# Another order of the first two head pairs: score banks for the second pair's transposes, VectorE for the first pair's low parts, k on ScalarE's queue

## The chip, the cores and the metric

The kernel runs on one core of a Trainium2 chip. The metric is the device time of one execution in microseconds (us). TensorE (PE) multiplies matrices, VectorE (DVE), ScalarE (ACT) and GpSimd (POOL) work on elements, SyncE (SP) issues transfers. Each engine works through its own list of instructions in order and waits on semaphores of the others.

## The reference

```python
# attention in clusters: q, k, v of 2 batches x 8 heads x 768 rows x 64
q_assign = argmax(einsum('bhsd,hcd->bhsc', q_n, c_n))      # 16 clusters; rows are normalised
k_assign = argmax(einsum('bhsd,hcd->bhsc', k_n, c_n))
mask = q_assign[:, :, :, None] == k_assign[:, :, None, :]
scores = where(mask, scale * q @ k.T, -1e9)
attn = exp(scores - max) / sum ; attn_out = attn @ v
x = attn_out as 1536 x 512
h = x @ w_in ; x = (h - tanh(h)) @ w_out                   # d_ff 2048
out = (sigmoid(x @ w_gate) * (x @ w_val)) @ w_out          # d_ff 1536
```

## The kernel before, in words

Sixteen heads are worked on as eight pairs; after them come the two feed-forward blocks. Every factor is split into a high part (rounded to the format that TensorE reads at full rate) and a low part (the rest), and a product is the sum of high x high, high x low and low x high.

`pair_prep` (a pair's preparation) loads q and k of two heads (L717), transposes them on TensorE (L728), copies the transposed halves to SBUF on ScalarE (`evac`, L732), and multiplies them by the normalised centroids on TensorE (`score`, L782). VectorE turns these cluster scores into one-hot rows (`assign`, L791 to L802), and TensorE transposes the one-hot rows (L873 in the first pair, L833 later). For the first pair ScalarE writes the high parts (`cast`, L746) straight into the operand tile of each head, `stk`, and POOL subtracts them for the low parts (L751); ScalarE adds the one-hot rows (L877). For later pairs high and low parts go to `hlq` and `hlk` (L758, L768) and SP copies them into `stk` (L466). v is scaled by a power of two (`v_scale`, L681 to L689, L923, L926).

A head's scores stand in a bank of PSUM ("big": `ba`, `bb`, later `bc`), one bank for each 128 rows, six in a head. A head is treated in one of two ways by the digit in `TURN`. Head 0 has digit 1: scores (L1013), maximum on VectorE (L1021), two exponentials on ScalarE (L1016, to float32 and to float16), the low part on POOL or VectorE (L1032), a transposing transfer (L1035), and the product with v (L1044 to L1046). All other heads first get their maxima from a product of high parts alone (`head_max`: L946 on TensorE, L950 on VectorE), which are turned into a row (L959, L965), and then scores with the maximum subtracted (L1066), exponentials (L1069), the low part (L1080) and the product with v (L1092 to L1094).

Small results use four other banks of PSUM: `smr` (three slots, in use at the start, the first NR pairs) and `sm`. When the last user of `smr` is done (`ramp`, `first_over`), its banks become the third big bank `bc` and one more `sm`. `keep_busy` (L659) puts matmuls on a tile of zeros into TensorE's list; they compute nothing that is used.

The order of all this is made when the program is built: a planner gives every task a place by a table of due times (`ORDER`, some 3,500 numbers), the look-ahead of each engine (`AH_...`) and the free tiles. A task takes its tile from the slot whose name is in its `take`. So a changed table moves every instruction, while what is computed stays.

The feed-forward blocks take their results from halved banks (`over_left`, `over_right`, `sm`); their products are L1379 and L1742, and with EU=1 the first ones are recorded one by one (L1446). `pair_of` splits results into high and low parts, a share GV or GW of the low parts on VectorE; W1L, D1L, W2L and D2L say how early weights are loaded.

```python
    for i in range(N_BUSY):
        fill.append(add(PE, 0.111, 1e6, keep_busy, fill[-1:], tail=0.055))
...
        smk = "smr" if s < NR else "sm"
...
            both = Slot("big") if s < PRM["TB"] else None
...
                on_v = x < PRM["NDV"]
```

Of the kernel before, what the change touches and what calls it, by code (L numbers as in the profile page):

```python
# [26 lines left out]
PRM = dict(  # L27
    QUEUE=2.4, AH_PE=0.1219, AH_ACT=0.29, AH_DVE=0.0344, AH_POOL=5.5247, AH_SP=2.0746, N_BUSY=110, NR=2, NRH=1,
    HX=['hx', 'hhxx'], WAR=0.8, LM=9, LV=9, ZP1=-12.307, ZP=1.419, FD=0.1631, FO=0.8005, LOQ=0, VHI=0,
    ZV0=-23.288, VR=40.471, ZSV=-53.844, ZRAW=10.895, ZT=1.445, ZH=70.02, ZHL=13.774, ZS=6.68, ZC=-1.658,  # L30
    ZOT=-19.503, ZD=22.333, ZDH=1.004, ZDM=4.532, ZVL=13.784, ZVS=23.559, ZX=-17.9, ZE=25.348, ZLOW=35.365,
    ZLOWP=0.736, SEMS=1.0, TC=0.58, TW=0.9, M2=1, ZQK=0.347, ZMS=-68.272, Z0=47.754, HB=93.143, NB4=5,
    ROWS=0.0155, NHA=8, RAWL=1.6, NMID=2, NPL=2, XB=0, XT=1, GV=0.1258, GW=0, NPL2=1, W1L=0.556, D1L=0.31,
    W2L=1.628, D2L=-0.119, ZI=18.277, ZJ=-10.865, PORT=0.12, PVG=1, NSPL=1, NRE=1.056, TURN='1000000000000000',
    ZMX=20.689, ZTR=9.194, TRL=2.05, TRC=1.4, ZPT=0.419, PVT=2, HD=0, HDO=0.0751, HC=0, HCO=0, ZHC=-56.991,
    NAT=2, TB=1, ZN=2.791, ZNL=-12.734, NDV=0, EU=1, ZUD=-29.266, ZU=-22.481, ZUS=-19.807, NEW=0, ZEW=-3.275)
# [1909 lines left out]
```

## Time and profile before

| | |
|---|---|
| time, median of 3 runs | 777.66 us (776.62 to 778.03) |
| profiled execution | 776.54 us, span 774.8 us |
| TensorE busy | 767.1 us (99%), 5905 matmuls |
| VectorE, ScalarE, GpSimd busy | 568.4, 457.6, 569.9 us |
| matmuls on zeros (L659) | 220, 16.6 us busy |

A matmul's end is modelled, and the next one starts before it, so a group's busy time and the distance of its starts are two things: six score products of 128 rows by 384 columns last 1.3 us in the timeline, and the next instruction starts about 1.1 us after the first. Times in the views count from the start of the span. The profiled execution is longer than its span by 1.8 us, and 1.1 us below the median of the runs.

### The profile page before, as it was taken

The page shows a single profiled execution, that of the slowest core. Times are in us where ns is not written, and L with a number is a line of the kernel's source. Part 1 is how long each engine was busy: PE and PEld are TensorE (multiplying, and loading weights), DVE is VectorE, ACT ScalarE, POOL GpSimd, SP SyncE. Part 2 cuts the span into 40 slices and gives each one's busy share as a digit, 9 for nine tenths or more (in the row PEclk, how much of TensorE's full clock was granted, in tenths as well). Part 3 has the DMA queues.
Part 4 walks back from the last instruction along what each step waited for, and adds up shares of the span by engine and source line. Part 5 has one row for each costly group of instructions (what it writes and reads, how often), then busy time and mean ns, then how long its engine had stood idle before and what let it go on. Part 6 is the DMA issues. An engine that isn't in the chain of part 4 may idle for free.

```text
span 774.8 us, 15780 instructions
## 1 busy us (share of the span) xinstructions
PE 767.1 (99%) x5905; PEld 725.4 (94%) x5905; DVE 568.4 (73%) x1111; ACT 457.6 (59%) x881; POOL 569.9 (74%) x604
## 2 busy tenths in 40 slices
PE   8999999999999999999999999999999999999998
PEld 7888999898899999999999999999998989899996
DVE  6797888788987977868577787795475796756324
ACT  6689997889996644644445455665552636254240
POOL 7368977878889874978778799698693888668231
PEclk9999999999999999999999999999999999999999
DMA  4797666575632100312122232012230242211004
GB/s 104 183 195 156 138 154 141 125 153 136 162 115 66 46 1 28 123 55 86 40 94 69 96 106 72 0 49 91 67 96 19 78 130 89 82 41 41 1 1 163
DMA packets 75572, 69.58 MB, mean 90 GB/s; under 512 B 39252, under 2 KB 60072, under 8 KB 75496
## 3 DMA queue, kind: packets, MB, share of 16 engines
q1 hardware_dynamic: 75352, 68.55, 33.0%
q8 instruction: 46, 0.75, 0.4%
q14 instruction: 30, 0.25, 0.1%
q10 hardware_dynamic: 144, 0.03, 0.0%
HBM read 45.12 MB, written 3.15 MB: 62 GB/s over the span
## 4 chain that ended last, share of the span: by engine, by line
PE 93%; DVE 3%; ACT 1%; issue 1%; DMA 1%; SPq 0%; DVEq 0%; ACTq 0%
PE over_left L1379 23%; PE over_left L1742 21%; PE over_right L1379 7%; PE over_right L1742 6%; PE sm L1379 6%; PE sm L1742 4%; PE bc L1066 3%; PE sm L782 2%; PE ba L1066 2%; PE bb L1066 2%; PE sm L1092 2%; PE sm L1093 2%; PE sm L1094 2%; PE ba L946 2%; PE bb L946 1%; PE sm L659 1%
## 5 line engine op out<-in xcount | busy, mean ns | idle before, releaser
L1080 POOL TENSOR_TENSOR pt<-pf,pt 128x768 f16<-128x768 f32 x46 | 77.5, 1695 | 17.7 <-ACT pf L1069 6.6
L1742 PE MATMUL over_left<-xh,stk 128*128 128x384 f32 x228 | 70.8, 336 | 0.0
L1762 DVE TENSOR_TENSOR pf<-over_left,pf 128x384 f32<-128x384 f32 x62 | 34.3, 554 | 40.2 <-ACT pf L1758 24.5
L1080 POOL TENSOR_TENSOR ptt<-pf,ptt 128x768 f16<-128x768 f32 x29 | 49.5, 1713 | 13.2 <-ACT pf L1069 10.8
L1410 ACT ACTIVATE hlk<-pf 128x384 fp32r<-128x384 f32 x44 | 22.9, 523 | 35.7 <-POOL pf L1772 13.7
L1379 PE MATMUL over_left<-hlk,w 128*128 128x384 f32 x154 | 43.4, 336 | 0.0
L1379 PE MATMUL over_left<-stk,w 128*128 128x384 f32 x138 | 43.2, 337 | 0.0
L1092 PE MATMUL sm<-vs,pt 128*128 128x65 f16 x318 | 42.9, 194 | 0.0
L1742 PEld LDWEIGHTS over_left<-xh,stk 128*128 128x128 f32 x228 | 42.3, 188 | 0.5
L1093 PE MATMUL sm<-vs,pt 128*128 128x64 f16 x318 | 42.8, 195 | 0.0
L1094 PE MATMUL sm<-vs,pt 128*128 128x65 f16 x318 | 42.4, 191 | 0.0
L1742 PE MATMUL over_left<-sum,stk 128*128 128x384 f32 x166 | 41.8, 336 | 0.2 <-ACT pf L1758 0.2
L1742 PE MATMUL over_left<-xh,ry 128*128 128x384 f32 x124 | 39.9, 336 | 0.0
L950 DVE TENSOR_REDUCE finr<-ba 128x1 fp32r<-128x768 f32 x35 | 33.2, 948 | 6.6 <-PE ba L946 3.9
L1412 POOL TENSOR_TENSOR hlq<-pf,hlk 128x384 fp32r<-128x384 f32 x25 | 25.8, 1032 | 16.1 <-ACT hlk L1410 16.1
L1758 ACT ACTIVATE pf<-over_left 128x384 f32<-128x384 f32 x44 | 21.4, 488 | 27.1 <-PE over_left L1742 27.1
L1379 PE MATMUL over_left<-w,stk 128*128 128x512 f32 (+1 forms) x108 | 37.0, 391 | 0.0
L1742 PE MATMUL over_left<-xl,stk 128*128 128x384 f32 x110 | 36.9, 336 | 0.0
L1497 DVE TENSOR_TENSOR ptt<-over_left,ptt 128x384 f32<-128x384 f32 x58 | 31.5, 550 | 6.8 <-PE over_left L1379 6.8
L1066 PE MATMUL bc<-stk 112*128 112x384 f32 (+2 forms) x150 | 34.7, 354 | 0.2 <-DVE finr L950 0.2
L1092 PEld LDWEIGHTS <-pt 128*128 128x128 f16 x318 | 29.7, 96 | 5.3 <-issue 4.9
L1353 POOL TENSOR_TENSOR w<-vs,w 128x256 fp32r<-128x256 f32 x25 | 19.8, 803 | 20.1 <-ACT w L1351 20.1
(600 smaller groups left out, 3056.8 us busy)
## 6 DMA issues: line engine op xcount, KB each, us to landing
vs<-in_moe_w_out_dram SPq DMA_DIRECT2D x48, 256.0 KB, 2.7
vs<-in_moe_w_in_dram SPq DMA_DIRECT2D x24, 256.0 KB, 2.6
vs<-in_moe_w_val_dram SPq DMA_DIRECT2D x24, 256.0 KB, 2.7
vs<-in_moe_w_gate_dram SPq DMA_DIRECT2D x24, 256.0 KB, 2.8
stk<-hlq SPq DMA_DIRECT2D x28, 192.0 KB, 2.6
stk<-hlk SPq DMA_DIRECT2D x14, 384.0 KB, 4.5
rawq<-in_q_dram SPq DMA_DIRECT2D x16, 192.0 KB, 3.5
rawk<-in_k_dram SPq DMA_DIRECT2D x16, 192.0 KB, 3.9
```

The costliest lines, as they stand in the source:

```text
L946: nc.tensor.matmul(at(mx)[:, j, 0:HALF], at(sk)[0:km, 0, t * P:(t + 1) * P], at(sk)[0:km, 1, j * HALF:(j + 1) * HALF], start=True, stop=True)
L950: rd.append(use(mx, add(DVE, c_dve(S), z + t, lambda t=t, mx=mx: nc.vector.tensor_reduce(at(mh)[:, t:t + 1], at(mx)[:, :, 0:HALF], axis=AX ...
L1066: nc.tensor.matmul(o, at(sk)[0:n, l_, ts], at(sk)[0:n, m_, c], start=i == 0, stop=i == len(terms) - 1)
L1080: lambda nce=nc.vector if on_v else nc.gpsimd, pf=pf, pt=pt: nce.tensor_tensor(at(pt)[:, 1], at(pf), at(pt)[:, 0], op=ALU.subtract), [e0, ...
L1092: nc.tensor.matmul(oview()[:, t], ph, vv[:, 0:D + 1], start=(kt == 0), stop=False)
L1093: nc.tensor.matmul(oview()[:, t, 0:D], ph, vv[:, D + 1:2 * D + 1], start=False, stop=False)
L1094: nc.tensor.matmul(oview()[:, t], plo, vv[:, 0:D + 1], start=False, stop=(kt == T - 1))
L1379: nc.tensor.matmul(ps, a, b, start=(i == 0), stop=(i == n - 1))
L1412: nc.vector if on_v else nc.gpsimd).tensor_tensor(lo(), src(), hi(), op=ALU.subtract), [a], port=True)
L1497: u = add(DVE, c_dve(CH), z, lambda a=a, src=src: nc.vector.tensor_tensor(a(), src(), a(), op=ALU.add), [t] + prev)
L1742: nc.tensor.matmul(at(bank[to])[:, 0:CH], lh, rh, start=start and i == 0, stop=stop and i == 3 * KH - 1, skip_group_check=True)
L1762: return use(x, use(bank[n], add(DVE, c_dve(CH), rank[0], lambda: nc.vector.tensor_tensor(at(x), ps(n), at(x), op=ALU.add), deps)))
```

## The change

Many constants of the planner and the whole table `ORDER` are other numbers, and three places of the code are different. N_BUSY goes from 110 to 5 (220 matmuls on zeros become 10). NR goes from 2 to 1 and TB from 1 to 2: the second pair's transposes of q and k go to the big banks, and its cluster scores and one-hot rows to `sm`. NDV goes from 0 to 2: the first pair's four low parts are made on VectorE. The first pair's k is loaded from ScalarE's queue. Z01 exchanges the operand tiles of heads 0 and 1. PVT goes from 2 to 1, EU from 1 to 0. The sizes and the number of all other matmuls stay.

```diff
-    QUEUE=2.4, AH_PE=0.1219, AH_ACT=0.29, AH_DVE=0.0344, AH_POOL=5.5247, AH_SP=2.0746, N_BUSY=110, NR=2, NRH=1,
+    QUEUE=2.4, AH_PE=0.1324, AH_ACT=0.2649, AH_DVE=0.025, AH_POOL=4.8207, AH_SP=1.1014, N_BUSY=5, NR=1, NRH=1,
...
-    ROWS=0.0155, NHA=8, RAWL=1.6, NMID=2, NPL=2, XB=0, XT=1, GV=0.1258, GW=0, NPL2=1, W1L=0.556, D1L=0.31,
-    W2L=1.628, D2L=-0.119, ZI=18.277, ZJ=-10.865, PORT=0.12, PVG=1, NSPL=1, NRE=1.056, TURN='1000000000000000',
-    ZMX=20.689, ZTR=9.194, TRL=2.05, TRC=1.4, ZPT=0.419, PVT=2, HD=0, HDO=0.0751, HC=0, HCO=0, ZHC=-56.991,
-    NAT=2, TB=1, ZN=2.791, ZNL=-12.734, NDV=0, EU=1, ZUD=-29.266, ZU=-22.481, ZUS=-19.807, NEW=0, ZEW=-3.275)
+    ROWS=0.0155, NHA=8, RAWL=1.6, NMID=2, NPL=2, XB=0, XT=1, GV=0.0854, GW=0.0192, NPL2=1, W1L=1.109,
+    D1L=-0.243, W2L=1.563, D2L=-0.377, ZI=-4.342, ZJ=-2.662, PORT=0.12, PVG=1, NSPL=1, NRE=1.056,
+    TURN='1000000000000000', ZMX=19.248, ZTR=4.682, TRL=2.05, TRC=1.4, ZPT=-0.489, PVT=1, HD=0, HDO=0, HC=0,
+    HCO=0.0306, ZHC=-58.936, NAT=2, TB=2, ZN=-8.697, ZNL=-81.82, NDV=2, Z01=1, EU=0, ZUD=-40.578, ZU=-8.093,
+    ZUS=-38.353, NEW=0, ZEW=-20.328)
...
     nc.scalar.dma_start(cn, centroids.rearrange("h c d -> (h c) d"))
+    for hh in range(2):
+        nc.scalar.dma_start(tiles["rawk", 0][:, :, hh], k[0, hh].rearrange("(p t) d -> p t d", t=T))
     nc.scalar.activation(warm, warm, AF.Sqrt)
...
-            ld = add(SP, 2 * DMA_C, z + PRM["ZRAW"] + x - (90 if s == 0 else 0), lambda load=load: (load(0), load(1)),
+            ld = add(SP, 2 * DMA_C, z + PRM["ZRAW"] + x - (90 if s == 0 else 0), (lambda: None) if s == 0 and x else lambda load=load: (load(0), load(1)),
                      take=[raw], lat=PRM["RAWL"])
```

What this makes of the order is shown at three places. In the changed kernel's file the same lines stand 6 to 8 numbers lower (L728 is L722, L782 is L776, L946 is L940, L1013 is L1007). The first is the start of TensorE's list, the matmuls on zeros and the weight loads left out. `ba` and `bb` are big banks, `rawq` and `rawk` the loaded q and k, `cn` the centroids, `vm` and `e` the scale of v. Before:

```order
L728 MATMUL ba_76<-ident,rawq_121 128x128 x3
L728 MATMUL bb_80<-ident,rawk_124 128x128 x3
L728 MATMUL ba_76<-ident,rawq_121 128x128 x3
L728 MATMUL bb_80<-ident,rawk_124 128x128 x3
L647 MATMUL smr_84<-ident,cn 64x128
L685 MATMUL smr_85<-ident,vm 1x128
L782 MATMUL sm_71<-cb,xtk_125 128x96 x3
L782 MATMUL smr_84<-cb,xtq_122 128x96 x6
L782 MATMUL sm_71<-cb,xtk_125 128x96 x3
L687 MATMUL smr_85<-e,ones_167 128x2
```

In the changed kernel:

```order
L722 MATMUL ba_76<-ident,rawq_121 128x128 x6
L722 MATMUL bb_80<-ident,rawk_124 128x128 x6
L641 MATMUL smr_84<-ident,cn 64x128
L679 MATMUL smr_85<-ident,vm 1x128
L776 MATMUL sm_71<-cb,xtq_122 128x96 x6
L722 MATMUL ba_76<-ident,rawq_121 128x128 x6
L681 MATMUL smr_85<-e,ones_167 128x2
L776 MATMUL smr_84<-cb,xtk_125 128x96 x6
L722 MATMUL bb_80<-ident,rawk_124 128x128 x6
L776 MATMUL sm_72<-cb,xtq_122 128x96 x6
L776 MATMUL sm_72<-cb,xtk_125 128x96 x6
```

The second pair's twelve transposes and its scores now stand between the first pair's scores and its one-hot rows; before, they stood behind the first pair's one-hot rows. (Each score matmul of this list is two in the trace.)

The second place is VectorE's list in the changed kernel, from the first scale of v to the first one-hot rows (`oh`). Before, it went from the copies of the centroids (`cb`) to the scale of v (`e`) and on to the maxima (`mm`) of the cluster scores.

```order
L675 TENSOR_REDUCE vm<-rawv_92 128x1
L646 COPY cb<-smr_84 64x4x16 x2
L745 TENSOR_TENSOR stk_86<-xtq_122,stk_86 64x768
L745 TENSOR_TENSOR stk_87<-xtq_122,stk_87 64x768
L670 TENSOR_REDUCE e<-smr_85 1x1
L671 TENSOR_SCALAR e<-e 1x1
L672 TENSOR_SCALAR e<-e 1x1
L673 RECIPROCAL e<-e 1x1
L745 TENSOR_TENSOR stk_87<-xtk_125,stk_87 64x768
L745 TENSOR_TENSOR stk_86<-xtk_125,stk_86 64x768
L683 TENSOR_SCALAR sv<-smr_85 128x1
L785 TENSOR_REDUCE mm_127<-sm_71 128x12
```

The four low parts (L745) now stand ahead of the first pair's assignment.

The third place is TensorE's list from head 0's first scores (L1007 on `stk_87`, before L1013 on `stk_86`) to head 1's maxima (L940, before L946). `bc` is the third big bank. In the changed kernel:

```order
L1007 MATMUL bb_80<-stk_87 128x384 x6
L679 MATMUL sm_71<-ident,vm 1x128
L940 MATMUL bc_372<-stk_86 128x384 x2
L722 MATMUL sm_72<-ident,rawk_124 128x128 x3
L940 MATMUL ba_76<-stk_86 128x384 x2
L681 MATMUL sm_71<-e,ones_167 128x2
L940 MATMUL bc_372<-stk_86 128x384 x2
L940 MATMUL bb_80<-stk_86 128x384 x2
```

Before:

```order
L946 MATMUL bb_80<-stk_87 128x384 x2
L685 MATMUL smr_84<-ident,vm 1x128
L946 MATMUL ba_76<-stk_87 128x384 x2
L687 MATMUL smr_84<-e,ones_167 128x2
L946 MATMUL bb_80<-stk_87 128x384 x2
L946 MATMUL ba_76<-stk_87 128x384 x2
L1013 MATMUL bb_80<-stk_86 128x384 x6
```

Head 1's maxima now use the third bank from their first row block; before, four of the six were made with two banks, and `bc` came with the sixth.

## Rows read from the trace of the kernel before

**Rows 1.** The page: busy time, share of the span and instructions of each engine.
```profile
PE 767.1 (99%) x5905; PEld 725.4 (94%) x5905; DVE 568.4 (73%) x1111; ACT 457.6 (59%) x881; POOL 569.9 (74%) x604
```
**Rows 2.** Busy time by stage: stretch, length, busy us (and instructions) of each engine.
```profile
22.00:37.00 15.00, 14.81 (x154) 13.26 (x154) 13.10 (x25) 8.74 (x13) 5.53 (x5) 1.00 0.78 169
50.00:225.00 175.00, 173.56 (x2267) 156.74 (x2266) 147.19 (x254) 152.95 (x230) 143.70 (x98) 1.00 0.62 144
225.00:235.00 10.00, 9.94 (x118) 9.47 (x116) 7.11 (x16) 9.79 (x17) 8.80 (x5) 1.00 0.39 133
235.00:771.70 536.70, 536.52 (x3060) 516.61 (x3056) 376.05 (x771) 260.43 (x585) 389.31 (x453) 1.00 0.20 65
```
**Rows 3.** TensorE in order of time, 0 to 60 us: start, length, what.
```profile
1.00 3.32 PE L659 MATMUL sm<-busy 128*128 128x128 bf16 x30 [1.00 <-DVE busy L584]
5.06 0.52 PE L728 MATMUL ba<-ident,rawq 128*128 128x128 f32 x3 [0.74 <-DMA rawq<-in_q_dram]
5.42 0.83 PE L659 MATMUL sm<-busy 128*128 128x128 bf16 x12
6.95 0.52 PE L728 MATMUL bb<-ident,rawk 128*128 128x128 f32 x3 [0.70 <-DMA rawk<-in_k_dram]
...
10.84 1.50 PE L782 MATMUL smr<-cb,xtq 128*128 128x96 f32 x12
...
19.81 1.31 PE L1013 MATMUL ba<-stk 80*128 80x384 f32 x6
...
32.11 0.84 PE L659 MATMUL sm<-busy 128*128 128x128 bf16 x12
...
36.69 0.82 PE L959 MATMUL bc<-ident,finr 128*1 128x128 f32 x6
```
**Rows 4.** TensorE's matmuls on zeros as a group.
```profile
L659 PE MATMUL sm<-busy 128*128 128x128 bf16 x220 | 16.6, 232 | 1.0 <-DVE busy L584 1.0
```
**Rows 5.** VectorE in order of time, 0 to 42 us.
```profile
9.53 0.45 DVE L652 COPY cb<-smr 64x64 f32<-64x64 f32 x2 [0.76 <-PE smr L647]
...
15.17 1.50 DVE L926 SCALAR_TENSOR_TENSOR vs<-rawv,sv,vs 128x384 f16<-128x384 f32 x1
16.59 0.34 DVE L802 TENSOR_TENSOR oh<-sm,mm 128x192 bf16<-128x192 f32 x1
16.86 1.90 DVE L926 SCALAR_TENSOR_TENSOR vs<-rawv,sv,vs 128x384 f16<-128x384 f32 x1
21.16 0.96 DVE L1021 TENSOR_REDUCE fin<-ba 128x1 f32<-128x768 f32 x1 [2.40 <-PE ba L1013]
...
30.62 0.60 DVE L926 SCALAR_TENSOR_TENSOR vs<-rawv,sv,vs 128x384 f16<-128x384 f32 x1
...
35.25 0.95 DVE L950 TENSOR_REDUCE finr<-bc 128x1 fp32r<-128x768 f32 x1
36.11 0.95 DVE L1032 TENSOR_TENSOR pt<-pf,pt 128x768 f16<-128x768 f32 x1
```
**Rows 6.** Busy time of the engines from the centroids' copies to head 1's last maximum.
```profile
9.50:36.20 26.70, 26.51 (x300) 24.14 (x298) 20.59 (x43) 17.45 (x28) 13.69 (x10) 1.00 0.63 140
```
**Rows 7.** ScalarE in order of time, 0 to 42 us.
```profile
3.80 0.20 ACT L630 ACTIVATE warm<-warm 1x1 f32<-1x1 f32 x1 [1.36 <-DVE warm L626]
...
9.77 0.83 ACT L746 ACTIVATE stk<-xtq 64x768 fp32r<-64x768 f32 x1
...
12.10 0.82 ACT L746 ACTIVATE stk<-xtk 64x768 fp32r<-64x768 f32 x1
```
**Rows 8.** POOL in order of time, 0 to 42 us.
```profile
14.45 3.90 POOL L751 TENSOR_TENSOR stk<-xtk,stk 64x768 fp32r<-64x768 f32 x2
```
**Rows 9.** SP's queue in order of time, 0 to 42 us.
```profile
2.19 1.34 SPq L717 DMA_DIRECT2D rawk<-in_k_dram  x2
3.58 0.64 SPq L918 DMA_DIRECT2D rawv<-in_v_dram  x1
```
**Rows 10.** Load of the transfers, 2.2 to 5.0 us; the last two numbers: share, GB/s.
```profile
2.20:5.00 2.80, 2.12 (x21) 1.91 (x18) 2.27 (x7) 1.22 (x4) 2.75 (x4) 1.00 1.00 221
```

More of the change, by code (lines that the diff above doesn't have):

```diff
@@ L27 @@
 PRM = dict(
-    QUEUE=2.4, AH_PE=0.1219, AH_ACT=0.29, AH_DVE=0.0344, AH_POOL=5.5247, AH_SP=2.0746, N_BUSY=110, NR=2, NRH=1,
[L29 to L32, printed above, removed]
-    ROWS=0.0155, NHA=8, RAWL=1.6, NMID=2, NPL=2, XB=0, XT=1, GV=0.1258, GW=0, NPL2=1, W1L=0.556, D1L=0.31,
-    W2L=1.628, D2L=-0.119, ZI=18.277, ZJ=-10.865, PORT=0.12, PVG=1, NSPL=1, NRE=1.056, TURN='1000000000000000',
-    ZMX=20.689, ZTR=9.194, TRL=2.05, TRC=1.4, ZPT=0.419, PVT=2, HD=0, HDO=0.0751, HC=0, HCO=0, ZHC=-56.991,
-    NAT=2, TB=1, ZN=2.791, ZNL=-12.734, NDV=0, EU=1, ZUD=-29.266, ZU=-22.481, ZUS=-19.807, NEW=0, ZEW=-3.275)
-ORDER = [int(x) for x in """
[204 rows of a table removed]
+    QUEUE=2.4, AH_PE=0.1324, AH_ACT=0.2649, AH_DVE=0.025, AH_POOL=4.8207, AH_SP=1.1014, N_BUSY=5, NR=1, NRH=1,
+    HX=['hx', 'hhxx'], WAR=0.8, LM=9, LV=9, ZP1=-19.548, ZP=1.492, FD=0.1631, FO=0.8005, LOQ=0, VHI=0,
+    ZV0=-14.061, VR=29.321, ZSV=-51.912, ZRAW=10.002, ZT=1.015, ZH=62.823, ZHL=13.598, ZS=6.621, ZC=3.839,
+    ZOT=-0.082, ZD=22.03, ZDH=5.63, ZDM=12.007, ZVL=18.661, ZVS=26.408, ZX=-45.885, ZE=11.865, ZLOW=30.819,
+    ZLOWP=2.901, SEMS=1.0, TC=0.58, TW=0.9, M2=1, ZQK=0.347, ZMS=-69.886, Z0=57.18, HB=93.79, NB4=5,
+    ROWS=0.0155, NHA=8, RAWL=1.6, NMID=2, NPL=2, XB=0, XT=1, GV=0.0854, GW=0.0192, NPL2=1, W1L=1.109,
[3 more added lines that the diff above has]
+    ZUS=-38.353, NEW=0, ZEW=-20.328)
+ORDER = [int(x) for x in """
[195 rows of a table added]
 """.split()]
@@ L607, in tile_cluster_attention_moe @@
     if PRM["NAT"]:
-        nc.vector.memset(tiles["stk", 0].bitcast(F32)[D:2 * D, 2:4].rearrange("p a n -> p (a n)"), 0.0)
-        nc.gpsimd.memset(tiles["stk", 1].bitcast(F32)[0:D].rearrange("p a n -> p (a n)"), 0.0)
-    for i in (2, 0) if PRM["NAT"] else range(NS):
+        nc.vector.memset(tiles["stk", PRM["Z01"]].bitcast(F32)[D:2 * D, 2:4].rearrange("p a n -> p (a n)"), 0.0)
+        nc.gpsimd.memset(tiles["stk", 1 - PRM["Z01"]].bitcast(F32)[0:D].rearrange("p a n -> p (a n)"), 0.0)
+    for i in (2, PRM["Z01"]) if PRM["NAT"] else range(NS):
         nc.gpsimd.memset(tiles["stk", i].bitcast(F32)[96:97, 3, :], 1.0)
@@ L744, in cast @@
                 def cast(xt=xt, sk=sk, rw=rw, x=x, hh=hh):
-                    assert sk.item == hh
+                    assert sk.item == (hh ^ PRM["Z01"])
                     nc.scalar.activation(at(sk)[rw, x], at(xt)[rw], AF.Copy)
```

399 rows, old and new, of the table ORDER are left out of this document.

## The prediction, made before the changed kernel ran

> **What bounds the kernel now.** I read the page first: TensorE is busy 99% of the span, no other engine over 75% [rows 1]. Next the busy time by stage: from 235 to 771.7 us TensorE sits idle for 0.2 us in all, from 50 to 225 us for 1.4 us [rows 2]. A feed-forward block can therefore give nothing back unless it loses matmuls, and its matmuls stay. But "busy" is no measure of use at the start. The timeline of TensorE shows matmuls on zeros between the real ones up to about 33 us [rows 3], 220 of them [rows 4]. From 22 to 37 us VectorE is busy 13.1 of 15 us [rows 2]: there TensorE waits for VectorE's maxima, and zeros fill the wait. So the time is set by how early the first 35 us let TensorE run on real work without a break. I compare one point in both orders: the turning of head 1's maxima, which now starts at 36.69 us [rows 3]. After it the order before has no more zeros.
>
> **The change, part by part.**
>
> *Matmuls on zeros.* 210 fewer, each 0.056 us from the next at full speed (twelve in 0.83 us, less the last one's own 0.22) [rows 3, 4]: 11.8 us less of busy time. By itself this is worth nothing, since they stand in waits. What they do is shown by the first thirty: 3.32 us, so 0.107 us apart, and the twelve after a pause of 0.74 us at half that [rows 3]. That is the level of 1.2 GHz before and of 2.4 GHz after three us of unbroken matmuls (the profile's clock column reads 1.00 there too [rows 10], so I go by distances). With ten of them TensorE is idle from about 2.1 us until q is there, and I take its real work at half speed until about 14 us.
>
> *k on ScalarE's queue.* Two issues of 0.67 us [rows 9] go ahead of ScalarE's first table load. ScalarE now idles 1.36 us at that point, for a small fill on VectorE [rows 7], and this hides them; without that cover they would cost 1.3 us. The transfers are no faster: the load from 2.2 to 5.0 us is already full at 221 GB/s [rows 10]. q and k are 0.79 MB, 3.6 us, so both arrive at about 5.8 us as they now share the lanes. Before, TensorE got q at 5.06 and k at 6.95 us [rows 3]. SP's queue loses two issues and sends v earlier (before: 3.58 us [rows 9]), and the second pair's q as soon as TensorE has read the first one's.
>
> *Low parts on VectorE.* POOL took four of 1.9 us each, the last ending at 18.35 us [rows 8]. The trace has no such subtraction on VectorE; the nearest row is one of 768 columns at 0.95 us, starting 0.86 us after its neighbour [rows 5], so 0.87 each, 3.5 us in all. They go ahead of the first pair's assignment. In return the two v operations that ran beside POOL took 1.50 and 1.90 us where a later one took 0.60 [rows 5]: 2.2 us come back, as POOL is now idle there.
>
> Now the chain. TensorE: twelve transposes at half speed (0.22 each) from 5.8 to 8.5 us, the centroids and v's maximum to 8.9. ScalarE: after the first k half (7.9 us) three copies of 0.39 and four casts of 0.78 (from 9.77 to 12.10 for three [rows 7]) end at 12.2. VectorE: centroids to 9.4, then four low parts, v's scale (0.75) and its broadcast (0.2) from 9.7 to 14.1. TensorE meanwhile: scores of q (twelve take 1.50 us at full speed [rows 3], 0.111 apart; 2.7 us at half) from 9.6 to 12.3, the second pair's q transposes to 13.6, then, rising to full speed, scores of k to 15.7, transposes of k (0.7) to 16.4, 24 scores of the second pair (2.7) to 19.1. VectorE: ten assignment steps at 0.27 apart, the two v operations (1.1) and some 0.5 of waiting end the first pair's one-hot rows at 18.4. Before, they ended at 16.9 [rows 5]. So head 0's first scores move from 19.81 [rows 3] to about 21.3, **1.5 us later**.
>
> From there it turns. Before, VectorE sat idle 2.40 us until head 0's first scores [rows 5], as the second pair's cluster scores came behind them; now these are done first and fill that wait. Its assignment (2.4 us) runs from 19.3 to 21.7 and v's maximum to 22.6. Up to head 1's last maximum there follow four maxima of head 0, six of head 1, one low part, each 0.87 apart [rows 5], and 1.9 us of small things and v: 11.5 us, 34.1 us, with 0.5 for waits 34.6. The third bank, open before head 1's first block, removes the alternation of two banks. The turning starts at 34.8 instead of 36.69 us: 1.9 us. And TensorE has by then done three transposes and the third pair's twelve q scores more than before: 0.33 + 1.34 = 1.7 us. **Together 3.6 us.**
>
> Bounds of this. Best: VectorE never waits. It was busy 20.59 us from 9.50 to 36.20 [rows 6]; plus 3.5 for low parts, plus 1.7 for the maximum and the low part that it has done more, less 2.2, is 23.6 us from 8.9, so 32.5 us; the gain is 5.7 us. Worst: half speed to the end of the second pair's scores, the first rival below.
>
> *Everything later.* PVT lets the first product with v start after one transposed tile; the other tiles come later in the list anyway: nothing. SP's transposing transfers for it now stand behind nine copies into head 2's operand (0.7 us each [rows 9]), ready at some 30 us and wanted at 41: nothing, a cover of ten. The 24 products of EU stay matmuls of the same size. At the hand-over to the feed-forward blocks the last low part needs 4.2 to 4.6 us after the last score and TensorE has 4.2 us of products there, so 0 to 0.4 us lost (now 0.06 idle in that stretch [rows 2]). Shares GV and GW and the weight dates touch engines that are idle 27% and more of the time from 235 us on [rows 2]: nothing; if weights came late, the cost has no row, and I allow 0 to 2 us. In 50 to 225 us the new order may wait more or less than the 1.4 us of now: from 1 us gained to 2.6 lost (that is 1.5% of the stretch).
>
> Sum: 776.5 of the profiled execution less 3.6, plus 0.2 for the hand-over, is 773.1. The median of the runs shown is 1.1 above that execution, so the forecast for the median is 774.1; I write **774.0**.
>
> **The rivals.**
>
> *TensorE stays at half speed (slower).* For it: with ten zeros there is a gap of over 3 us ahead of q and gaps behind it, and before, thirty unbroken matmuls went ahead of the rise [rows 3]. Against it: from 9.6 us on the list is unbroken. If the half level lasts to the end of the second pair's scores, k's scores end at 16.9 instead of 15.7, k's transposes at 18.2, the 24 scores at 23.6 instead of 19.1, and the one-hot transposes (24) take 1.4 us more: 5.9 us later, no gain of 3.6 but a loss of 2.3, 780.0. It decides where the second pair's scores start 0.22 us apart instead of 0.11; lasting to 17 us costs about 2 us and leaves 776.
> The Trainium skill, "TensorE: Matmul & The Clock Gate", section on what is actually happening with the clock gate, speaks for this rival: there the throttled level is the default and activity releases it, and an idle spell brings it back. By that rule the zeros are what a start full of waits needs, and the sum would be 780; whether the trace agrees past the first pause cannot be seen before, since the zeros hide it.
>
> *The start gains and the attention gives it back.* VectorE, ScalarE and POOL are busy 84, 87 and 82% from 50 to 225 us [rows 2], and TensorE waits there only where a list places a matmul ahead of its data. A new list can lose the 2.6 us above and a weight 1 us: 777.7, no change. Against it: the same planner and the same work.
>
> *VectorE never waits.* 5.7 us: 772.0. Against it: what passes between engines in that stretch waited 0.76 and 2.40 us in the two rows that show it [rows 5].
>
> That the change doesn't do what it says is excluded by the order shown: ten zeros, four low parts on VectorE, transposes in the big banks.
>
> **How the numbers follow.** The forecast 0.50 (its own range 772.5 to 776), VectorE never waiting 0.14, gains given back 0.21, half speed 0.15. Three runs differ by 1.4 us, so 0.2%, 1.6 us, is what can be told from no change. Faster by more than that: 0.50 + 0.14, **0.64**; within it **0.21**; slower **0.15**. The range that leaves out half of the slow rival and the best end: **771.0 to 779.5**.
>
> **What would show it.** Right: the first twelve transposes 0.22 us apart and the second pair's scores 0.11; VectorE's L802 of the first pair (L796 there) later than before and its first head maximum right behind a gapless assignment; L959 (L953 there) near 34.8 us; idle time of TensorE up by some us in the first 35 us, since nothing fills its waits, and unchanged from 50 us on. Wrong: score matmuls 0.22 us apart past 17 us; head 1's last maximum after 36 us; waits of TensorE over 1.4 us in the attention or over 0.2 us in the feed-forward blocks.

## The result and the profile after

The change made the kernel slower: 785.6 us (median of 4, 783.73 to 786.78) against 777.85 us (4 runs, 776.62 to 778.15), a ratio of 1.0100, 95% interval 1.0088 to 1.0112. Forecast were 774.0 us and a range up to 779.5. The profiled execution took 785.49 us.

The page of the changed kernel, which answers to [rows 1]:

```profile
span 783.7 us, 15363 instructions
...
PE 762.9 (97%) x5695; PEld 717.7 (92%) x5695; DVE 574.7 (73%) x1117; ACT 457.7 (58%) x881; POOL 562.1 (72%) x598
```

TensorE has lost 210 matmuls on zeros, and still the span is 8.9 us longer. Busy time by stage, the same stretches as [rows 2] (the number behind POOL's is the granted clock):

```profile
22.00:37.00 15.00, 12.22 (x68) 10.43 (x66) 12.81 (x22) 8.91 (x14) 2.98 (x3) 0.89 0.73 155
50.00:225.00 175.00, 169.36 (x2139) 151.63 (x2138) 145.11 (x244) 147.25 (x221) 136.47 (x92) 0.99 0.62 142
225.00:235.00 10.00, 8.69 (x118) 7.93 (x116) 7.17 (x13) 8.32 (x13) 9.51 (x9) 1.00 0.18 54
```

In the attention, 50 to 225 us, TensorE now sits idle 5.6 us (before 1.4), at the hand-over 1.3 us (before 0.06). TensorE in order of time, from the start to the turn of head 1's maxima (L953, before L959):

```profile
1.00 1.25 PE L653 MATMUL sm<-busy 128*128 128x128 bf16 x10 [1.00 <-DVE busy L576]
6.20 1.51 PE L722 MATMUL ba<-ident,rawq 128*128 128x128 f32 x6 [3.95 <-POOL stk L603]
...
10.26 1.55 PE L776 MATMUL sm<-cb,xtq 128*128 128x96 f32 x12 [0.60 <-ACT xtq L726]
11.83 0.85 PE L722 MATMUL ba<-ident,rawq 128*128 128x128 f32 x6
...
16.26 1.48 PE L776 MATMUL sm<-cb,xtq 128*128 128x96 f32 x12
...
21.43 1.31 PE L1007 MATMUL ba<-stk 80*128 80x384 f32 x6 [0.20 <-ACT stk L871]
...
28.21 0.62 PE L940 MATMUL ba<-stk 128*128 128x384 f32 x2 [1.57 <-ACT pf L1010]
...
30.52 1.48 PE L722 MATMUL sm<-ident,rawq 128*128 128x128 f32 x6
...
37.36 0.82 PE L953 MATMUL ba<-ident,finr 128*1 128x128 f32 x6 [0.27 <-DVE finr L944]
```

The turn stands at 37.36 us, where 34.8 was forecast and 36.69 stood before [rows 3]. Six transposes take 1.48 us at 30.52, where six took 0.85 us at 11.83. What TensorE waited for, in the whole span (us in total, times, longest):

```profile
PE ba L722 <- POOL stk L603: 4.0, 1, 4.0
PE sm L959 <- DVE sv L683: 2.2, 1, 2.2
PE ba L940 <- ACT pf L1010: 1.6, 1, 1.6
PE sm L1120 <- DVE xnt L1105: 1.5, 2, 1.1
PE smr L681 <- DVE e L673: 1.2, 1, 1.2
```

The second is the largest behind the start. VectorE at the place of the third of them (first two lines) and of the second:

```profile
24.61 0.95 DVE L675 TENSOR_REDUCE vm<-rawv 128x1 f32<-128x768 f32 x1 [1.68 <-DMA rawv<-in_v_dram]
25.48 0.95 DVE L1015 TENSOR_REDUCE fin<-ba 128x1 f32<-128x768 f32 x1
...
118.81 5.50 DVE L1074 TENSOR_TENSOR pt<-pf,pt 128x768 f16<-128x768 f32 x1
124.23 0.14 DVE L683 TENSOR_SCALAR sv<-sm 128x1 f32<-128x1 f32 x1
```

A low part that takes 0.95 us elsewhere [rows 5] took 5.50. Behind it stood the small instruction that makes `sv`, and for that TensorE waited. POOL meanwhile:

```profile
117.02 6.47 POOL L1074 TENSOR_TENSOR pt<-pf,pt 128x768 f16<-128x768 f32 x4
```

Four low parts without a gap, the last of them ending at 123.5 us; VectorE's ended 0.8 us later. TensorE's clock in two stretches; they begin 1.7 and 1.0 us behind the end of such a wait:

```profile
29.90:33.30 3.40, 3.40 (x13) 3.30 (x14) 3.40 (x6) 2.20 (x5) 0.05 (x1) 0.50 0.66 119
...
125.50:128.80 3.30, 3.30 (x27) 3.04 (x27) 1.84 (x3) 1.97 (x3) 0.64 (x1) 0.50 0.37 78
```

Half speed, 0.50, in both; before, the clock stood at full from 4.1 us to the end. (In the changed kernel it first rose at 9.4 us.)

To compare stretches in which the order differs I use one measure. Each matmul that is not on zeros counts as much as the median distance to the next one that its shape has in the trace of before (0.175 us for 128x384, for instance). Added up in order of time these give the work done; it is 736.1 us in every kernel here. The time at which W us of work are done, less W, is what was lost by then; in the changed kernel 25 us of work are done at 43.7 us, 90 at 116.1 and 120 at 152.5. The columns by their labels are experiments of the next section (each from its profiled execution):

| W done | before | changed | e1 | e6 | e7 | e9 | e11 |
|---|---|---|---|---|---|---|---|
| 25 | 19.9 | 18.7 | 17.8 | 16.7 | 15.4 | 17.5 | 21.5 |
| 40 | 21.2 | 21.6 | 20.7 | 19.8 | 18.5 | 20.3 | 22.9 |
| 90 | 24.7 | 26.1 | 25.6 | 23.6 | 24.9 | 24.9 | 26.3 |
| 120 | 27.4 | 32.5 | 27.9 | 26.0 | 27.2 | 31.1 | 29.0 |
| 190 | 33.0 | 38.9 | 33.8 | 31.9 | 33.2 | 37.1 | 34.6 |
| 240 | 34.1 | 41.2 | 36.1 | 34.2 | 35.5 | 39.4 | 36.7 |
| 700 | 35.4 | 44.4 | 39.0 | 37.0 | 38.3 | 42.5 | 38.1 |

The 8.9 us of the two spans, stretch by stretch: the start gains 1.2; from 25 to 90 us of work 2.6 are lost, from 90 to 120 (the 5.50 us low part) 3.7, from 120 to 190 0.8, at the hand-over (190 to 240) 1.2, in the feed-forward blocks 1.8. Differences of 1 to 2 us at the start are no larger than those between executions: e11 keeps the order of before up to the hand-over and still stands 1.6 us behind it at 25 us of work.

### The profile page after: what moved, and what is told of

Read it like the earlier page. It is cut to its first block, busy times and chain, and to the rows that moved or that the text cites. A ratio compares the mean times of both kernels' runs of the same rounds, so it can differ in the third digit from the quotient of the medians.

```text
span 783.7 us, 15363 instructions
## 1 busy us (share of the span) xinstructions
PE 762.9 (97%) x5695; PEld 717.7 (92%) x5695; DVE 574.7 (73%) x1117; ACT 457.7 (58%) x881; POOL 562.1 (72%) x598
## 4 chain that ended last, share of the span: by engine, by line
PE 88%; DVE 5%; ACT 3%; DMA 2%; issue 1%; POOL 1%; SPq 0%; DVEq 0%; ACTq 0%; POOLq 0%
PE over_left L1373 18%; PE over_left L1736 17%; PE sm L1373 11%; PE sm L1736 10%; PE over_right L1373 8%; PE over_right L1736 5%; PE bb L1060 3%; PE bc L1060 2%; PE sm L1086 2%; PE sm L1087 2%; PE ba L1060 2%; PE sm L1088 2%; DVE finr L944 2%; PE ba L940 1%; PE bb L940 1%
## 5 line engine op out<-in xcount | busy, mean ns | idle before, releaser
L1074 POOL TENSOR_TENSOR pt<-pf,pt 128x768 f16<-128x768 f32 x45 | 75.5, 1694 | 24.7 <-ACT pf L1063 10.2
L1756 DVE TENSOR_TENSOR pf<-over_left,pf 128x384 f32<-128x384 f32 x44 | 24.2, 553 | 26.1 <-ACT pf L1752 13.5
L1087 PE MATMUL sm<-vs,pt 128*128 128x64 f16 x318 | 38.3, 195 | 0.0
L1088 PE MATMUL sm<-vs,pt 128*128 128x65 f16 x318 | 38.1, 191 | 0.0
L1406 POOL TENSOR_TENSOR oht<-pf,hlk 128x384 fp32r<-128x384 f32 x18 | 19.7, 1097 | 23.5 <-ACT hlk L1404 23.5
L1736 PE MATMUL over_left<-xh,stk 128*128 128x384 f32 x116 | 36.2, 336 | 0.0
L1347 POOL TENSOR_TENSOR stk<-ry,w 128x256 fp32r<-128x256 f32 x33 | 25.4, 782 | 13.7 <-ACT w L1345 13.4
L1373 PE MATMUL over_left<-stk,stk 128*128 128x384 f32 (+1 forms) x106 | 34.3, 354 | 0.0
L1060 PE MATMUL bb<-stk 112*128 112x384 f32 (+2 forms) x144 | 33.3, 354 | 0.8 <-DVE finr L944 0.4
L1086 PEld LDWEIGHTS <-pt 128*128 128x128 f16 x318 | 29.4, 96 | 4.5 <-issue 4.4
L1063 ACT ACTIVATE pf<-bb 128x768 f32<-128x768 f32 x35 | 28.7, 820 | 2.8 <-PE bb L1060 1.9
L944 DVE TENSOR_REDUCE finr<-bc 128x1 fp32r<-128x768 f32 x25 | 23.7, 948 | 8.9 <-PE bc L940 8.6
L1063 ACT ACTIVATE pf<-bc 128x768 f32<-128x768 f32 x32 | 26.1, 817 | 6.8 <-PE bc L1060 5.9
L1088 PEld LDWEIGHTS <-pt 128*128 128x128 f16 x318 | 30.0, 99 | 0.0
L1736 PE MATMUL over_left<-xh,w 128*128 128x384 f32 x96 | 29.9, 338 | 0.0
L1087 PEld LDWEIGHTS <-pt 128*128 128x128 f16 x318 | 29.8, 97 | 0.1
```

Source lines behind the costliest of these rows:

```text
L944: rd.append(use(mx, add(DVE, c_dve(S), z + t, lambda t=t, mx=mx: nc.vector.tensor_reduce(at(mh)[:, t:t + 1], at(mx)[:, :, 0:HALF], axis=AX ...
L1060: nc.tensor.matmul(o, at(sk)[0:n, l_, ts], at(sk)[0:n, m_, c], start=i == 0, stop=i == len(terms) - 1)
L1063: nc.scalar.activation(o.rearrange("p (j n) -> p j n", j=2), at(st)[:, :, 0:HALF], AF.Exp)
L1074: lambda nce=nc.vector if on_v else nc.gpsimd, pf=pf, pt=pt: nce.tensor_tensor(at(pt)[:, 1], at(pf), at(pt)[:, 0], op=ALU.subtract), [e0, ...
L1086: nc.tensor.matmul(oview()[:, t], ph, vv[:, 0:D + 1], start=(kt == 0), stop=False)
L1087: nc.tensor.matmul(oview()[:, t, 0:D], ph, vv[:, D + 1:2 * D + 1], start=False, stop=False)
```

## The experiments

The theory after the result (A): the loss lies in the newly drawn order of the attention, its largest piece the low part at 118.8 us. Its rivals: (B) the missing zeros and the clock at half at the start; (C) the edits themselves. In all runs but for the named edit every engine keeps its order: the plan is made as it was and only what a step emits is changed. Ratios are to the kernel before, run beside it on the same chip.

**e1: that one low part on POOL.**

```
- nce=nc.vector if on_v else nc.gpsimd
+ nce=nc.vector if on_v and n != 38 else nc.gpsimd
```

> The changed kernel in the same order, but the one low part that took 5.50 us on VectorE (tile 38) is issued on GpSimd. Theory A (the loss lies in the order of the attention, and this low part is its largest piece): the 2.2 us wait for sv at 122 us and the 3.4 us at half clock behind it go, together 2.4 + 1.7 = 4.1 us: 781 to 782.5 us. Theory B (the missing zeros and the half clock at the start cost the time) and theory C (the edits of the first 20 us cost it): no change, 785 to 786 us. If another wait stands behind this one, GpSimd's queue being one low part (1.65 us) longer there, A gains less than 2 us.

Measured: 780.12 us (779.71 to 780.83), ratio 1.0038 (1.0023 to 1.0053). Of the 7.75 us over the kernel before, 3.11 are left: 4.6 us went (5.5 between the two medians, which were taken beside different executions of the kernel before). That is a little more than A had put on it. VectorE then sits waiting for TensorE where it was shut in before, and POOL does six low parts in a row:

```profile
120.27 0.16 DVE L683 TENSOR_SCALAR sv<-sm 128x1 f32<-128x1 f32 x1 [1.90 <-PE sm L681]
```
```profile
116.55 9.69 POOL L1074 TENSOR_TENSOR pt<-pf,pt 128x768 f16<-128x768 f32 x6
```

The wait for `sv` is gone, and so is the half clock behind it. The table gives the stretch itself: from 90 to 120 us of work the loss is 2.3 us instead of 6.4. That is 4.1 us, what was expected; the rest is a better start in this execution (0.9) and spread. A holds for its largest piece.

**e2: the kernel before with two edits of the start** (k on ScalarE's queue, four low parts of the first pair on VectorE), and **e5: the first of them alone.**

```
+ for hh in range(2):
+     nc.scalar.dma_start(tiles["rawk", 0][:, :, hh], k[0, hh]...)
- lambda load=load: (load(0), load(1))
+ (lambda: None) if s == 0 and x else lambda load=load: (load(0), load(1))
```
```
- nce=nc.vector if on_v else nc.gpsimd     (e2 only, first pair's low parts)
+ nce=nc.vector
```

> The kernel before, its order of work unchanged on every engine but for two edits of the change: the first pair's k is issued from ScalarE's queue, and all four low parts of the first pair run on VectorE instead of GpSimd. Theory A (the newly drawn order costs the time): 776 to 778.5 us, for the old order's later steps stay and little waits for the edits. Theory C (the edits themselves cost it): 782 us or more.

> The kernel before, order unchanged, with one edit alone: the first pair's k is issued from ScalarE's queue, and so v's load stands 1.4 us earlier on SP's. Theory D (the three loads share the DMA engines, so q lands about 1.1 us later, and the longer wait keeps TensorE's clock at half until about 9.8 us): most of the 3.8 us that both edits cost together, 779 to 780.5 us, with q's transposes at 6.2 us instead of 5.06. Rival (the low parts on VectorE were the costly edit): 777 to 778 us.

Measured: e2 780.79 us, ratio 1.0047 (1.0030 to 1.0064); e5 779.36 us, ratio 1.0022 (1.0012 to 1.0031). Neither theory had e2 right: in the old order the edits cost 3.8 us. About half is k's queue: e5 lies in D's range, though D spoke of most. TensorE at the start of e5:

```profile
1.00 3.38 PE L661 MATMUL sm<-busy 128*128 128x128 bf16 x30 [1.00 <-DVE busy L584]
6.07 0.88 PE L730 MATMUL ba<-ident,rawq 128*128 128x128 f32 x3 [1.69 <-DMA rawq<-in_q_dram]
```

q's transposes start at 6.07 instead of 5.06 us [rows 3], though nothing of q's own transfer was touched; the likely reason is that k and the earlier v now take their part of a load that was already full [rows 10]. The other profiles agree, where at most 42 zeros stand ahead: with k on ScalarE's queue q's transposes start at 6.07 to 7.12 us (six profiles), with k on SP's queue at 5.03 to 5.45 us (five). The clock rose at 9.6 instead of 4.1 us in e5, but the longer wait is not why it missed the early rise: at 4.1 us both kernels were still in the same thirty matmuls on zeros. e11, with k on SP's queue, rose at 10.3 us and lost 1.6 us more than the kernel before by 25 us of work, as much as e5. So how much of the 1.8 us is q's delay and how much the clock is not shown. Of the other half, on e2's low parts, the trace shows 1.2 us: with them on VectorE TensorE waited 0.7 and 0.5 us for the one-hot rows.

**e3: the kernel before without 210 of its zeros; e4: the changed kernel with zeros put back.**

```
- fill.append(add(PE, ..., keep_busy, ...))                              (e3)
+ fill.append(add(PE, ..., keep_busy if i < 5 else lambda: None, ...))
```
```
- for _ in range(2):      + for _ in range(10):                          (e4, keep_busy)
+ zeros(at(sc)[:, 2 * P:3 * P], 14 if s == 1 else 0)       ahead of vm's turn
+ zeros(at(sc)[:, 2 * P:3 * P], 0 if s else 18)            ahead of e's product
+ if s == 2 and x and half == 0: zeros(at(sm)[:, 384:512], 26)
```

> The kernel before, order unchanged, with 10 of the 220 multiplications by zeros kept. Theory A: half clock until about 9 us and again after the waits of 1 to 1.3 us that the zeros filled, 1 to 3 us in all: 778.5 to 781 us. Theory B (the zeros are what the change loses): 784 us or more, with the clock at half in several stretches behind 50 us too.

> The changed kernel, order unchanged, with zeros put back: 50 at the start, 18 in the 1.2 us wait for e at 12.7 us, 14 ahead of vm's turn at 24.8 us and 26 behind the third pair's first k transposes at 26.6 us. Theory A: the clock is full from about 4 us and no longer falls at 29.9 us, which gives back at most 1.7 us there and up to 1 us of the transposes at 6 to 9 us: 783 to 785 us, with the waits at 122 and 230 us unchanged. Theory B: 778 to 780 us.

Measured: e3 784.22 us (782.79 to 786.44), ratio 1.0093 (1.0069 to 1.0116); e4 786.74 us (786.1 to 791.21), ratio 1.0135 (1.0106 to 1.0164). The zeros are worth 7 us in the old order, far over the 1 to 3 expected under A; it is the time that B gave, without the half clock behind 50 us that B spoke of. In the profiled execution the clock stayed at half until 24.1 us and fell again. From 31 to 41 us:

```profile
31.00:41.00 10.00, 9.36 (x32) 7.64 (x33) 7.78 (x14) 4.11 (x6) 1.70 (x2) 0.50 0.68 130
```

In the new order they are worth nothing, against B and against A's one or two us; by its distance to the kernel before e4 is 2 us slower than the changed kernel. The clock was full from 6.4 us, fell at 33.7 instead of 29.9 us, and the low part took its time as before:

```profile
120.39 5.52 DVE L1080 TENSOR_TENSOR pt<-pf,pt 128x768 f16<-128x768 f32 x1
```

So the zeros are not what the change lost; but a start full of waits needs them, unless, as here, its work was drawn together first.

**e8: the low part left on VectorE, but behind `sv`.**

```
  def v_sv():
      nc.vector.tensor_scalar(sv[:, s:s + 1], ...)
+     while held_low:
+         held_low.pop()(now=True)     (the low part of n == 38, held back)
```

> The changed kernel with tile 38's low part left on VectorE but placed behind the 0.14 us instruction that makes sv, instead of ahead of it. Theory A (VectorE's low part is shut out while GpSimd runs low parts without a gap, and the 2.2 us of TensorE are the queue behind it): the wait for sv at 122 us goes, the low part still lasts 3 to 5 us, and now the row maxima behind it are late, with a wait of 1 to 2 us for a score bank: 782 to 784.5 us. Rival (the length of that low part is an accident of when it starts): it lasts 1 to 2 us, and all of the 5.5 us come back, 780 us.

Measured: 784.84 us (782.72 to 787.22), ratio 1.0096 (1.0072 to 1.0119). VectorE:

```profile
122.24 0.16 DVE L684 TENSOR_SCALAR sv<-sm 128x1 f32<-128x1 f32 x1 [1.90 <-PE sm L681]
122.32 3.78 DVE L1081 TENSOR_TENSOR pt<-pf,pt 128x768 f16<-128x768 f32 x1
126.03 0.94 DVE L948 TENSOR_REDUCE finr<-ba 128x1 fp32r<-128x768 f32 x1
```

and TensorE's wait has only changed its name:

```profile
PE ba L944 <- DVE finr L948: 3.4, 3, 2.5
```

The low part began 3.5 us into POOL's run (118.83 to 125.3 us; in the changed kernel 1.8 us into it) and again ended 0.8 us after the run. So here the run set its end, not its start, against the rival. But not every run does. In the kernel before:

```profile
145.37 1.65 DVE L1080 TENSOR_TENSOR ptt<-pf,ptt 128x768 f16<-128x768 f32 x1
```
```profile
144.54 1.65 POOL L1080 TENSOR_TENSOR pt<-pf,pt 128x768 f16<-128x768 f32 x1
146.16 2.37 POOL L1080 TENSOR_TENSOR ptt<-pf,ptt 128x768 f16<-128x768 f32 x1
148.48 1.65 POOL L1080 TENSOR_TENSOR pt<-pf,pt 128x768 f16<-128x768 f32 x1
```

Again POOL has no gap, but VectorE's low part ended 0.8 us behind the first of the three, and POOL's second took 0.7 us longer. What decides which of the two happens is open. As to the time, A had the mechanism of e8 (another wait takes the place of the one for `sv`) but put that wait at 1 to 2 us; it was 2.5, and of the 7.75 us over the kernel before only 0.4 went. Order on VectorE alone hardly helps; the loss is the shut-out.

**e6: e1 with k on SP's queue again; e7: and 50 zeros at the start.** (The two edits are those of e5 undone and `range(10)` of e4.)

> The changed kernel with tile 38's low part on GpSimd (780.1 us as measured) and the first pair's k loaded from SP's queue again, between q and v. Theory D: q's first transposes at 5.1 instead of 6.1 us and k's at 6.9 instead of 7.7, so 0.8 to 1.1 us less: 779 to 779.5 us. Rival (the start is set by ScalarE's and VectorE's chain behind, or the gain is given back at the waits of 25 to 33 us): 780 us as it was.

> As the run with the low part on GpSimd and k on SP's queue, and 50 multiplications by zeros at the start instead of 10. Theory D with the clock: q's, k's and the first scores' 54 matmuls run at full clock, 1.5 to 2.5 us less than without the zeros: 777 to 778 us, no faster than the kernel before. Rival (zeros at the start change nothing, as they did in the changed kernel itself): 779 to 780 us.

Measured: e6 781.85 us (ten runs, 778.1 to 785.14), ratio 1.0057 (1.0040 to 1.0075); e7 779.61 us (778.09 to 786.42), ratio 1.0033 (1.0012 to 1.0055). By the medians D missed both; e7 lies in its rival's range, though 2.2 us below e6. The profiled executions (778.10 and 779.44 us) show the expected start: q's transposes at 5.07 us in e6, and by 25 us of work e6 stands 3.2 and e7 4.5 us ahead of the kernel before (table). By 90 us of work that lead is 1.1 and -0.2 us (e7 had 3.4 us at half clock from 67.5 us, behind a wait of 1.1 us). So e7 had a start better than the 3.6 us that I forecast, and the attention took it back. And executions of one kernel lie 7 to 8 us apart.

**e9: head 0's first maximum ahead of vm; e10: e7 with four such moves; e13: e7 with three of them.**

```
+ for n, before in [(62, 203)]:        (e9: L1015 on ba ahead of L675)
+     x = next(x for x in order if x[1].n == n)
+     order.remove(x)
+     order.insert(next(i for i, y in enumerate(order) if y[1].n == before), x)
```
```
  e13: [(62, 203), (109, 209), (113, 71)]     e10: the same and (1205, 1077)
```

> The changed kernel with one instruction moved on VectorE: head 0's first maximum (L1015 on ba) ahead of the second pair's vm (L675), which stands 1.68 us idle for v's load with that maximum behind it. Theory E (between 22 and 37 us the loss is VectorE's order, in which a wait for a transfer stands ahead of the maximum that frees the first score bank): ba is read at 22.8 instead of 25.5 us, the 1.57 us wait of TensorE at 28.2 us goes, its clock does not fall at 29.9 us, and 1.5 to 3 us of 785.6 are gone: 782.5 to 784 us. Rival (VectorE is full from 24.6 to 37 us whatever comes first): the turn of head 1's maxima stays at 37 us, no change.

> The fastest start so far (low part on GpSimd, k on SP's queue, 50 zeros; 779.6 us as measured) with four instructions moved ahead: head 0's first maximum ahead of vm, head 1's maximum of bb ahead of the two low parts of v, head 1's maximum of ba ahead of head 0's low part, and at the hand-over one tile's scores ahead of the xnt transposes that wait 1.1 us for VectorE. Theory E: 0.7 + 0.4 us of the waits at 29 to 32 us and 0.9 of the 1.3 us at 224.5 us go: 777 to 778.5 us. Rival (each wait removed comes back at the next bank): 779.6 us as before. Faster than the kernel before, under 776 us, under neither.

> The version with low part on GpSimd, k on SP's queue, 50 zeros and the three moves on VectorE, but without the move at the hand-over, which in the profile of the four moves took 1.1 us more between 190 and 240 us of work. If VectorE's order at 22 to 32 us is what is left of the start's loss, 777.5 to 779 us; if executions with the clock at half in the stretches of 36 to 50 us come again, as with the four moves, a median of 780 us or more and a spread of over 4 us. That it beats the kernel before (under 776.5 us) neither theory expects.

Measured: e9 783.96 us (783.08 to 785.68), ratio 1.0082 (1.0066 to 1.0097); e10 783.22 us (779.17 to 787.14), ratio 1.0064 (1.0038 to 1.0089); e13 783.06 us (777.87 to 787.34), ratio 1.0063 (1.0029 to 1.0096). In e9 the 1.57 us wait and the half clock of 29.9 us are gone, and the turn of head 1's maxima comes at 36.07 us:

```profile
23.49 0.95 DVE L1019 TENSOR_REDUCE fin<-ba 128x1 f32<-128x768 f32 x1
24.36 0.94 DVE L679 TENSOR_REDUCE vm<-rawv 128x1 f32<-128x768 f32 x1
```
```profile
36.07 0.81 PE L957 MATMUL ba<-ident,finr 128*1 128x128 f32 x6 [0.34 <-DVE finr L948]
```

That is 1.3 us earlier, and 1.6 us of the median (1.3 by the distance to the kernel before), as E expected. The rival has a part in it too: between 28 and 36.1 us TensorE still waits four times for VectorE's maxima, 0.3 to 0.6 us each. And from 25 to 90 us of work e9 loses 7.4 us, as the changed kernel does (before 4.8). e10 and e13 bring no more: e10 missed all that was expected of it, e13 has the median and the spread that it gave for the case of half clock; the move at the hand-over in e10 made that stretch longer (3.4 us from 190 to 240, e7 2.3). What they show is the clock. The executions of e13 by their mean granted clock: 777.87 and 778.13 us at 1.000, 780.55 at 0.997, 783.42 at 0.996, 783.06 at 0.993, 786.71 and 787.34 at 0.989. In the profiled one of e10:

```profile
36.00:50.00 14.00, 13.94 (x77) 12.67 (x78) 8.70 (x14) 6.59 (x10) 6.55 (x4) 0.51 1.00 193
```

0.989 of 787 us is 17 us at half clock, 8.7 us of work; that is nearly the whole distance to 778. The order is the same, so whether the clock falls differs from one execution to the next. (The mean leaves out the start up to the first rise: e8's profile reads 0.998 with half speed up to 18.6 us. And it does not explain every slow execution: e6's slowest, 785.14 us, stands at 0.998.) The kernel before stood at 0.998 or more in every execution beside these, the changed one at 0.993 to 0.998.

**e11: the kernel before with its early feed-forward matmuls issued together**, as a stand-in for EU=0.

```
- for i, (a, b) in enumerate(...):
+ for kk in range(KD) if kk == KD - 1 else ():
+     for i, (a, b) in enumerate(...):
```

> The kernel before, order unchanged, but the early piece of the feed-forward (24 matmuls of L1446, of the share that EU sets) is no longer spread in pieces of 3 between the last heads' steps at 224 to 241 us: each group of 12 is issued together where its last piece stood. Theory F (the hand-over of the changed kernel loses 1.2 us because the spread filler is gone): 0.8 to 1.5 us more, 778.3 to 779 us. Rival (other work fills TensorE there): no change within 0.3 us.

Measured: 778.64 us, ratio 1.0009 (1.0000 to 1.0017). In the trace the stretch from 190 to 240 us of work costs 2.1 us instead of 1.1, with a wait that the kernel before has not:

```profile
PE sm L1126 <- DVE xtq L1326: 0.7, 1, 0.7
```

F is supported by the trace (1.0 us, the changed kernel loses 1.2 there), by the medians only just.

**e12: the kernel before with 24 more zeros in its first two waits.**

```
- keep_busy                 + lambda i=i: keep_busy(14 if i in (14, 20) else 2)
```

> The kernel before, order unchanged, with 24 more multiplications by zeros: 12 ahead of q's first transposes, where TensorE waits 0.74 us for the load, and 12 ahead of k's, where it waits 0.70 us. Theory G (in the kernel before too the clock's rise hangs on these waits: full from 4.1 us where they are short, and only from 9.6 to 10.3 us in the profiled runs with a wait of 1.0 to 1.8 us): the clock is full from 4.1 us in every execution, the slower executions of 778 to 779 us go, median 776.5 to 777.2 us. Rival (the zeros delay q's and k's transposes as much as the clock gives back): 777.5 to 778.5 us.

Measured: 778.75 us, ratio 1.0010 (1.0002 to 1.0019): G fell; its rival, up to 778.5 us, came nearest. The zeros ran at half speed and stood in q's way:

```profile
1.00 4.66 PE L659 MATMUL sm<-busy 128*128 128x128 bf16 x42 [1.00 <-DVE busy L584]
5.45 0.87 PE L728 MATMUL ba<-ident,rawq 128*128 128x128 f32 x3
```

The clock was full from 6.5 us here, from 10.3 us in e11 with the zeros of before unchanged, and from 4.1 us in the profile of before. When it rises is no constant of the order.

No version beat the kernel before. Of the 7.8 us between the medians, 4 to 5.5 go with e1's one instruction, 1.3 to 1.6 with e9's, about 1 with what e11 imitates; the pieces overlap and don't simply add. Two pieces are open. The 2.6 us between 25 and 90 us of work are lost in every version of the new order in the table (2.1 us or more against the kernel before); the profile of the changed kernel shows only waits of 0.4 us and less there. The 1.8 us of the feed-forward blocks lie in many small pieces, in a stretch (235 to 771.7 us) in which TensorE is idle for 0.04 us, and nothing was tried on them.

## Why the prediction was wrong

Forecast were 3.4 us gained in the profiled execution, and 8.9 us were lost. Of the 12.3 us between, 2.4 stand in the start, 7.1 in the attention (25 to 190 us of work), 1.0 at the hand-over and 1.8 in the feed-forward blocks.

*The start's chain.* Head 0's first scores came at 21.43 us, forecast 21.3, but this is luck: two errors cancel. VectorE:

```profile
11.15 1.94 DVE L745 TENSOR_TENSOR stk<-xtq,stk 64x768 fp32r<-64x768 f32 x2 [1.04 <-ACT stk L740]
...
19.59 0.36 DVE L796 TENSOR_TENSOR oh<-smr,mm 128x192 bf16<-128x192 f32 x1
...
22.31 0.62 DVE L796 TENSOR_TENSOR oh<-sm,mm 128x192 bf16<-128x192 f32 x2
...
36.36 0.94 DVE L944 TENSOR_REDUCE finr<-ba 128x1 fp32r<-128x768 f32 x1
```

The low parts began at 11.15 us, behind a wait of 1.04 us for ScalarE's cast that the forecast has not, and the first pair's one-hot rows ended at 19.95 us, not 18.4. From there to head 0's scores took 1.5 us; the forecast had carried over the 2.9 us of before. That the first transposes run at half speed (0.21 apart) and the second pair's scores at full speed (24 from 16.26 us on, 0.11 apart) was right: the clock rose at 9.4 us, even before the 14 that I took, so that the first pair's q scores too ran at full speed (12 in 1.55 us from 10.26 us on, forecast 2.7). The rival of half speed did not come in its form. What the Trainium skill says there, "TensorE: Matmul & The Clock Gate", section on what is actually happening, that idleness brings the lower level back, the trace shows later: at 29.9 and 125.5 us, behind waits of 1.57 and 2.2 us. But in e8 the same wait of 1.57 us was followed by no fall. q was there at 6.2 us, not 5.8; I had left out v, which is on its way then as well.

*"Up to head 1's last maximum there follow four maxima ..., 11.5 us".* This held: from head 0's first maximum at 25.48 us to the end of head 1's last at 37.30 us are 11.8 us, where 11.5 and 0.5 of waits were forecast. What failed stands ahead of it: the second pair's assignment ended at 22.93 us, not 21.7, and v's maximum, which I had end at 22.6, waited 1.68 us for v's load and ended at 25.56. I had given that load no date. The turn came at 37.36 instead of 34.8 us (e9: 1.3 us of it), and the clock fell once more at 29.9 us. Instead of 3.6 us the start gave 1.2 by 25 us of work and none by 40.

*"In 50 to 225 us the new order may wait more or less than the 1.4 us of now: from 1 us gained to 2.6 lost".* **This is the step that failed most.** TensorE's idle time there went from 1.4 to 5.6 us, and 3.4 us at half clock cost another 1.7: 5.9 us lost, of which 4.1 hang on one instruction (e1). The bound of 2.6 was 1.5% of the stretch, a share without a mechanism. The rival "the start gains and the attention gives it back" named the right place, and e7 shows it even with a better start; but it was priced by that bound, and the way in which VectorE loses to POOL was in the rows: I credited 2.2 us for two operations that ran long beside POOL [rows 5] and did not ask where the new order puts such pairs next.
The Trainium skill, "SBUF — State Buffer", section on the two separate sides, has a rule for it: a VectorE operation with two inputs in SBUF and a GpSimd operation that reads SBUF take a shared port pair as an exclusive lock, for the whole instruction, and the other one is blocked. The trace agrees as to the blocking: in the kernel before, VectorE's low part at 145.37 us ended 0.8 us behind the POOL instruction that it met. In the run of four it went further: in the profiles of the changed kernel, e4, e9 and e8 (5.50, 5.52, 5.51 and 3.78 us) VectorE was not let in between POOL's instructions either, but only behind the last. That it is this lock is the Trainium skill's word; the runs show the times.

*The hand-over.* "0 to 0.4 us lost" was 1.2. That the 24 products of EU "stay matmuls of the same size" is true, but spread in pieces of three they filled waits (e11).

*Zeros.* "By itself this is worth nothing, since they stand in waits": in the new order that held (e4), in the old one it was wrong by 7 us (e3), with the clock at half up to 24.1 us and from 31 to 41 us.

*The feed-forward blocks* were costed at nothing, with 0 to 2 us allowed for late weights, and lost 1.8 us; TensorE shows no waits there, so the cause stays open.

Two of the signs that the prediction named for being wrong came true: head 1's last maximum after 36 us, and a wait of over 1.4 us in the attention. Its sum has a slip that changes nothing: 773.1 and 1.1 are 774.2.

## What to carry to other kernels

Where two engines share the element-wise work of a stage, look for the places where one runs several such instructions back to back, and ask what it costs if the other's large instruction there lasts as long as the whole series. Giving it to the engine of the series took most of that cost away (e1); only putting the short, waited-for instruction ahead of it did not, as the next one behind it was waited for too (e8). A wait for a transfer at the head of an engine's list costs what stands behind it: ask for each such wait what could go first. And a gain at the start can be lost again in the waits of the next stage (e7); price a redrawn order by its own waits, not by those of the old one.

## What the runs showed of the hardware

- A low part on VectorE (128x768, two inputs in SBUF) that met a run of four POOL low parts ended 0.8 us behind the run's last, whether it began 1.8 or 3.5 us into the run: 5.50 and 3.78 us instead of 0.95. In another run without a gap (kernel before, 145.37 us) it ended 0.8 us behind the first, after 1.65 us, and POOL's next took 2.37 us instead of 1.65.
- TensorE's granted clock fell to half for 3.4 us at each of the four waits of 2.2 to 2.5 us for VectorE near 125 us (changed kernel, e4, e8, e9), behind a wait of 1.57 us in the changed kernel and of 1.1 us in e7 and e13, and for 13.7 us in the profiled execution of e10. It did not fall behind waits of 1.57 us (e8), 1.56 us (e4, at 94.7 us) and 1.41 us (e6). In one and the same order (e13) it fell in some executions and not in others, 778 to 787 us.
- With the same 30 matmuls on zeros from 1.0 us on, the clock was full from 4.1 us, while they still ran, in the profile of before, and only from 9.6 to 10.3 us in those of e5, e2 and e11.
- With k issued from ScalarE's queue at 1.16 us, between the issues of q's two halves on SP's, and v 1.4 us earlier, q's transposes began 1.0 us later (e5).
